# A new written order from the second group on, and one store per row tile, in a linear attention and FFN kernel

## The chip, the cores and the metric

The kernel runs on one core of a Trainium2 chip. The metric is the device time of one execution in microseconds, median over runs. Engine names are those of the profile: PE (TensorE, matmuls; PEld is its weight load), DVE (VectorE), ACT (ScalarE), POOL (GpSimd) and SP (SyncE, which here only issues DMAs; SPq is its queue).

## What is computed

A lightning (linear, decaying) attention over `q, k, v` of shape (4, 8, 768, 64), and behind it an FFN with a "snake" activation over its 3072 rows of 512. Cut to what matters:

```python
for b in range(nb):                       # blocks of 64 positions
    intra = einsum('bhic,bhjc->bhij', qb, kb) * Dmask
    intra = einsum('bhij,bhjd->bhid', intra, vb)
    inter = einsum('bhid,bhde->bhie', qb * lam_pow, kv_state)
    out[:, :, sl] = intra + inter
    kv_state = lam_block * kv_state + einsum('bhsd,bhse->bhde', kb * rev_pow, vb)

x = out.transpose(0, 2, 1, 3).reshape(B * S, H * D)        # 3072 x 512
h = x @ w_in                                               # 512 -> 2048
g = h + sin(alpha * h) ** 2 / (alpha + 1e-9)
return g @ w_out                                           # 2048 -> 512
```

## The kernel before

**Tiling.** The kernel takes chunks of 128 positions, in windows of 256. A *unit* is one batch entry, one half of the heads (4 of 8) and one window; there are 24. Four units (two batch entries, two halves of the heads) make a *group* of 512 rows; there are 6 groups, 0 to 5, and group g holds units 4g to 4g+3. Attention makes the group's transposed activations `xt`; FFN1 turns them into 16 tiles of hidden features (`f`), each 128 x 512, in PSUM; sine, square and a last VectorE step (`snake`) make `gall` of them; FFN2 makes four row tiles (`m`) of 128 rows of output from the 16, in four parts (`j`) of four matmuls each.

A chunk's 128 positions are loaded as 64 pairs (`two`), so position 2i lies on partition i of the half `par` 0 and position 2i+1 on partition i of the half 1. In the kernel before, this order of the positions is kept up to the output: a row tile holds the even rows on partitions 0 to 63 and the odd ones on 64 to 127.

**The written order.** There is no scheduler at run time and none at build time: `ORDER` (L18 to L128) is a list of items that are issued one after the other, each to one engine, and each engine works through its own items in that order. Waits come from the data and from buffers that have to come free. An item is `name.indices:engine:banks`, with V for VectorE, A for ScalarE, G for GpSimd, T for TensorE and S for SyncE. The names, with the lines of the kernel before:

| item | what it is | line |
|---|---|---|
| `ld.u.j` | load of q, k or v (j) of unit u, 256 KB | L259 |
| `sq`, `sk`, `cv` | scale q (QL), scale k (KD), cast v (VB), to bf16 | L300, L282/L284 |
| `tq`, `tk`, `tcq`, `tck` | transposes on TensorE (units 0 to 7) and their copies to QT | L327, L282/L284 |
| `tdq`, `tdk` | the same as DMA transposes from SP's queue (units 8 to 23) | L345 |
| `s`, `m.u.h` | scores, 64x64 matmuls into banks s0 and s1; their masking | L368, L378 |
| `k`, `kc`, `a`, `n` | K-by-V sums (`kvp`), their copy, the sum with the state (kvx) and its spread form (kvbd), the next state | L400, L282/L284, L421 and L425, L433 |
| `oi`, `o`, `x.u.c` | product with the state, with the masked scores, both into banks oa and ob; eviction into `xt` | L446, L460, L471 |
| `f1a`, `f1` | FFN1: `f1a` is the first half of the columns (first two units), `f1` the rest or all | L482 |
| `sin`, `sqr`, `stt` | sine, square, snake | L502, L509/L511, L516 |
| `f2.g.m.j`, `oc.g.m`, `st` | FFN2, copy of a row tile to an output buffer `ob`, its store | L525, L282/L284, L540 |
| `w.n:bank` | n warm-up matmuls on zeros, 256 columns each | L588 |
| `lt.i`, `ltc.i` | the last row tile, in three column pieces of 256, 128 and 128: matmuls, copy and store | L550, L560 |

**What ties them.** PSUM has eight banks (h0 to h3, s0, s1, oa, ob, numbered 0 to 7 in the items), each holding one tile at a time: a matmul into a bank waits until the tile before it in that bank has been read. The load buffers hold 8 units, KD and VB 5, QL and QT 4; there are 4 output buffers, which are reused in the order in which their stores stand. All loads, all DMA transposes and nearly all stores stand in SP's one queue; w_in and w_out come from GpSimd's. The loads of unit 4 and later are held until FFN1 tile 12 of group 0 (`HOLD`).

Of the kernel before, what the change touches and what calls it, by code (L numbers as in the profile page):

```python
# [18 lines left out]
tab:V ld.0.0:S sq.0:V ap:T w.4:T:h0 tq.0:T:0 ld.0.1:S ld.0.2:S sk.0:V cv.0:A w.3:T:h1 tk.0:T:5 al:V  # L19
tck.0:V ld.1.0:S ld.1.1:S ld.1.2:S ld.2.0:S ld.2.1:S ld.2.2:S ld.3.0:S tcq.0:A k.0:T:1,2 a.0.0:V  # L20
w.4:T:oa s.0:T sq.1:G sk.1:G sq.2:G kc.0.0:A kc.0.1:V m.0.0:V w.3:T:oa tq.1:T:2 w.3:T:oa tk.1:T:4
cv.1:A tcq.1:A k.1:T:0,1 oi.0:T m.0.1:V o.0:T x.0.0:A x.0.1:A tck.1:V kc.1.0:V kc.1.1:A a.1.0:V
s.1:T sk.2:V cv.2:A w.5:T:h2 tq.2:T:6 tk.2:T:1 w.2:T:h2 k.2:T:2,0 ld.3.1:S m.1.0:V m.1.1:V kc.2.0:V
kc.2.1:V wi.0:G wi.1:G a.2.0:V sq.3:G sk.3:G n.2.0:G wi.2:G n.0.0:G tcq.2:A w.1:T:ob oi.1:T tck.2:A
ld.3.2:S o.1:T x.1.0:A x.1.1:A cv.3:A s.2:T tq.3:T:1 w.4:T:oa oi.2:T tk.3:T:0 w.2:T:h2 k.3:T:2,3
m.2.0:V m.2.1:V o.2:T tck.3:V wi.3:G wo.0:G wo.1:G tcq.3:A s.3:T x.2.0:A a.3.0:V kc.3.0:V m.3.0:V
x.2.1:A m.3.1:V w.6:T:h1 oi.3:T f1a.0.0:T:0 f1a.0.1:T:4 o.3:T x.3.0:A kc.3.1:V f1a.0.2:T:3
f1a.0.3:T:2 wo.2:G x.3.1:V f1.0.0:T f1.0.1:T sin.0.0:A sin.0.1:A f1.0.2:T sqr.0.0:V stt.0.0:V
sqr.0.1:G stt.0.1:V f1.0.3:T f1.0.4:T:5 f1.0.5:T:7 sin.0.2:A sin.0.3:A sqr.0.2:A stt.0.2:V sqr.0.3:A
sin.0.4:A sqr.0.4:V sin.0.5:A f1.0.6:T:1 stt.0.3:V sin.0.6:A sqr.0.5:G f1.0.7:T:6 stt.0.4:V  # L30
f1.0.8:T:0 sqr.0.6:V stt.0.5:V stt.0.6:V f1.0.9:T:2 f1.0.10:T:4 f1.0.11:T:3 sin.0.7:A sin.0.8:A
sqr.0.7:G stt.0.7:V sqr.0.8:A stt.0.8:V n.1.0:G sin.0.9:A sqr.0.9:V a.1.1:G stt.0.9:V sin.0.10:A
sqr.0.10:G sin.0.11:A sqr.0.11:V f1.0.12:T:1 sin.0.12:A sqr.0.12:A a.0.1:G wo.3:G a.2.1:G n.2.1:G
stt.0.10:V stt.0.11:V f1.0.13:T:5 f1.0.14:T:7 sin.0.13:A sin.0.14:A n.0.1:G n.1.1:G n.3.0:G ld.4.0:S
ld.4.1:S ld.4.2:S ld.5.0:S ld.5.1:S ld.5.2:S ld.6.0:S sqr.0.13:V stt.0.12:V stt.0.13:V sqr.0.14:A
stt.0.14:V ld.6.1:S ld.6.2:S ld.7.0:S ld.7.1:S ld.7.2:S ld.8.0:S ld.8.1:S f2.0.0.0:T:0 f1.0.15:T:2
f2.0.0.1:T f2.0.1.0:T:6 sq.4:G f2.0.3.0:T:3 sin.0.15:A sqr.0.15:V f2.0.2.0:T:1 f2.0.1.1:T f2.0.2.1:T
stt.0.15:V f2.0.2.2:T f2.0.0.2:T f2.0.0.3:T f2.0.3.1:T oc.0.0:V a.3.1:G sk.4:G tq.4:T:7 tk.4:T:2
ld.8.2:S ld.9.0:S ld.9.1:S ld.9.2:S tck.4:V tcq.4:A f2.0.1.2:T s.4:T ld.10.0:S cv.4:A sq.5:G
tq.5:T:0 sk.5:G sq.6:G tcq.5:A f2.0.1.3:T oc.0.1:A sk.6:G tk.5:T:2 cv.5:G m.4.0:V f2.0.3.2:T m.4.1:V  # L40
k.4:T:6,7 a.4.0:V tck.5:A s.5:T m.5.0:V tq.6:T:0 cv.6:A tcq.6:V kc.4.0:A tk.6:T:2 m.5.1:V kc.4.1:A
ld.10.1:S ld.10.2:S f2.0.2.3:T tck.6:A oi.4:T k.5:T:0,2 o.4:T oc.0.2:A x.4.0:A x.4.1:A sq.7:G sk.7:G
s.6:T a.5.0:V kc.5.0:A kc.5.1:A f2.0.3.3:T tq.7:T:1 m.6.0:V m.6.1:V tcq.7:V cv.7:G n.3.1:G oi.5:T
oc.0.3:A sq.8:G tk.7:T:4 n.4.0:G sk.8:G tck.7:V a.4.1:G o.5:T k.6:T:0,2 k.7:T:1,3 x.5.0:A x.5.1:A
s.7:T n.5.0:G tdq.8:S a.6.0:V w.2:T:oa oi.6:T kc.6.0:A o.6:T a.7.0:V f1a.1.0:T:0 x.6.0:A m.7.0:V
n.4.1:G ld.11.0:S tdk.8:S ld.11.1:S x.6.1:A kc.6.1:V f1a.1.1:T:2 cv.8:A kc.7.0:A m.7.1:V oi.7:T
o.7:T k.8:T:4,5 f1a.1.2:T:1 x.7.0:V x.7.1:A f1.1.0:T f1.1.1:T f1.1.2:T kc.8.0:A sq.9:G f1a.1.3:T:4
f1.1.3:T kc.7.1:A f1.1.4:T:7 sin.1.0:A sin.1.1:A sin.1.2:A sk.9:G ld.11.2:S sqr.1.0:V stt.1.0:V
sin.1.3:A cv.9:A sqr.1.1:G stt.1.1:V sq.10:G sin.1.4:A sqr.1.2:V sqr.1.3:A stt.1.2:V stt.1.3:V
kc.8.1:V f1.1.5:T:3 sin.1.5:A f1.1.6:T:0 sqr.1.4:G sqr.1.5:G f1.1.7:T:6 f1.1.8:T:1 k.9:T:4,5  # L50
sin.1.6:A stt.1.4:V stt.1.5:V sin.1.7:A f1.1.9:T:2 kc.9.0:V sqr.1.6:A f1.1.10:T:7 kc.9.1:A sqr.1.7:A
tdq.9:S s.8:T a.8.0:G sk.10:G st.0.0.0:S ld.12.0:S tdk.9:S st.0.0.1:S stt.1.6:V stt.1.7:V sin.1.8:A
sqr.1.8:A sin.1.9:A sin.1.10:A stt.1.8:V m.8.0:V f1.1.11:T:3 f1.1.12:T:0 f1.1.13:T:1 sq.11:G
tdq.10:S sin.1.11:A f1.1.14:T:4 ld.12.1:S ld.12.2:S ld.13.0:S sqr.1.9:V sqr.1.10:A sqr.1.11:G
stt.1.9:V stt.1.10:V sin.1.12:A sqr.1.12:G sin.1.13:A stt.1.11:V stt.1.12:V m.8.1:V sk.11:G
f1.1.15:T:2 cv.10:G sin.1.14:A sqr.1.13:A oi.8:T sin.1.15:A tdk.10:S f2.1.0.0:T:3 sqr.1.14:A sk.12:G
sq.12:G f2.1.0.1:T f2.1.0.2:T a.9.0:G sqr.1.15:A cv.11:A stt.1.13:V stt.1.14:V stt.1.15:V s.9:T
o.8:T tdq.11:S ld.13.1:S ld.13.2:S k.10:T:0,1 x.8.0:A x.8.1:A m.9.0:V tdk.11:S f2.1.0.3:T m.9.1:V
oi.9:T kc.10.0:A st.0.1.0:S ld.14.0:S kc.10.1:A o.9:T cv.12:A x.9.0:A s.10:T k.11:T:2,0 f2.1.1.0:T:1
m.10.0:V a.10.0:G x.9.1:A kc.11.0:A kc.11.1:A m.10.1:V oi.10:T k.12:T:2,0 n.6.0:G n.8.0:G n.9.0:G  # L60
s.11:T o.10:T kc.12.0:V f2.1.1.1:T ld.14.1:S m.11.0:V ld.14.2:S n.10.0:G x.10.0:V m.11.1:V
f2.1.1.2:T ld.15.0:S st.0.1.1:S ld.15.1:S tdq.12:S ld.15.2:S ld.16.0:S ld.16.1:S ld.16.2:S ld.17.0:S
oc.1.0:A kc.12.1:A x.10.1:A a.11.0:G sk.13:G cv.13:G oi.11:T o.11:T x.11.0:A sq.13:G f2.1.1.3:T
sq.14:G oc.1.1:A n.7.0:G x.11.1:V f1.2.0:T:6 sin.2.0:A f1.2.1:T:5 sin.2.1:A sqr.2.0:A stt.2.0:V
ld.17.1:S st.1.1.0:S a.6.1:G n.6.1:G sk.14:G ld.17.2:S st.0.3.0:S st.0.2.0:S f1.2.2:T:2 sin.2.2:A
sqr.2.1:A stt.2.1:V f1.2.3:T:7 sin.2.3:A f1.2.4:T:0 f1.2.5:T:3 sin.2.4:A f1.2.6:T:4 f1.2.7:T:5
sqr.2.2:G stt.2.2:V sqr.2.3:A a.5.1:G stt.2.3:V sin.2.5:A f1.2.8:T:6 f1.2.9:T:7 f1.2.10:T:1 sq.15:G
sk.15:G sqr.2.4:A sin.2.6:A sqr.2.5:A stt.2.4:V f2.1.2.0:T:0 stt.2.5:V cv.14:G f1.2.11:T:3 tdk.12:S
f1.2.12:T:2 sin.2.7:A f2.1.2.1:T st.0.2.1:S sin.2.8:A sqr.2.6:G sqr.2.7:A stt.2.6:V sin.2.9:A
stt.2.7:V sqr.2.8:G sin.2.10:A n.11.0:G stt.2.8:V sqr.2.9:A sqr.2.10:A stt.2.9:V stt.2.10:V sq.16:G  # L70
sin.2.11:A sqr.2.11:A tdq.13:S n.5.1:G tdk.13:S tdq.14:S st.0.3.1:S tdk.14:S a.7.1:G a.12.0:G s.12:T
k.13:T:6,7 kc.13.0:A sin.2.12:A kc.13.1:A sqr.2.12:A m.12.0:V m.12.1:V tdq.15:S f1.2.13:T:1
f2.1.2.2:T sin.2.13:A sqr.2.13:A oi.12:T s.13:T o.12:T stt.2.11:V f2.1.2.3:T a.13.0:G m.13.0:V
stt.2.12:V m.13.1:V stt.2.13:V x.12.0:A x.12.1:A f2.1.3.0:T:3 n.13.0:G n.7.1:G a.8.1:G oi.13:T
sk.16:G oc.1.2:A f1.2.14:T:2 o.13:T k.14:T:1,0 s.14:T sin.2.14:A x.13.0:V x.13.1:V m.14.0:V n.8.1:G
sq.17:G n.12.0:G kc.14.0:A f2.1.3.1:T m.14.1:V f2.1.3.2:T sqr.2.14:A a.14.0:G kc.14.1:A tdk.15:S
ld.18.0:S ld.18.1:S oi.14:T ld.18.2:S sq.18:G cv.15:A cv.16:G cv.17:A k.15:T:1,0 o.14:T s.15:T
tdq.16:S tdk.16:S stt.2.14:V kc.15.0:V x.14.0:V x.14.1:A f1.2.15:T:2 f2.1.3.3:T st.1.2.0:S a.15.0:G
m.15.0:V kc.15.1:V oi.15:T m.15.1:V ld.19.0:S ld.19.1:S ld.19.2:S s.16:T ld.20.0:S st.1.0.0:S o.15:T
x.15.0:V k.16:T:1 x.15.1:V sin.2.15:A sqr.2.15:A m.16.0:V oc.1.3:V stt.2.15:V a.11.1:G f2.2.0.0:T:0  # L80
f1.3.0:T:7 kc.16.0:A st.1.0.1:S ld.20.1:S m.16.1:V sin.3.0:A sqr.3.0:A f1.3.1:T:4 f1.3.2:T:6
sin.3.1:A f1.3.3:T:1 sqr.3.1:A sin.3.2:A sin.3.3:A f1.3.4:T:5 sin.3.4:A f1.3.5:T:2 f1.3.6:T:3
sk.17:G st.1.2.1:S ld.20.2:S sk.18:G sk.19:G f2.2.0.1:T f2.2.0.2:T a.9.1:G sq.19:G sq.20:G sqr.3.2:G
stt.3.0:V sqr.3.3:A stt.3.1:V a.16.0:G n.9.1:G sin.3.5:A sqr.3.4:A stt.3.2:V n.14.0:G n.15.0:G
sin.3.6:A stt.3.3:V stt.3.4:V sqr.3.5:A ld.21.0:S tdq.17:S tdk.17:S sqr.3.6:A cv.18:G tdq.18:S
tdk.18:S st.1.3.0:S f1.3.7:T:1 oi.16:T stt.3.5:V a.10.1:G s.17:T o.16:T x.16.0:V k.17:T:2 f2.2.0.3:T
cv.19:G m.17.0:V stt.3.6:V x.16.1:V kc.17.0:A f2.2.1.0:T:2 a.17.0:G n.10.1:G n.11.1:G sk.20:G
cv.20:G a.12.1:G f2.2.1.1:T tdq.19:S ld.21.1:S tdk.19:S ld.21.2:S ld.22.0:S st.1.1.1:S tdq.20:S
ld.22.1:S tdk.20:S m.17.1:V oi.17:T oc.2.0:V s.18:T st.1.3.1:S k.18:T:3 k.19:T:0 o.17:T kc.18.0:A
# [41 lines left out]
def kernel(  # L131
# [11 lines left out]
    nc = tc.nc  # L143
    P = nc.NUM_PARTITIONS

    B, H, S, D = q.shape
    C = 128
# [234 lines left out]
    okv = {}  # L382
# [243 lines left out]
```

## Time and profile before

| what | us |
|---|---|
| six runs: 215.9, 216.45, 216.68, 214.27, 215.25, 216.06; median | 215.98 |
| the profiled execution's own time | 214.85 |
| its span, first to last instruction | 213.1 |
| PE busy | 206.1 |
| POOL busy | 141.4 |
| DVE busy | 129.6 |
| ACT busy | 123.6 |
| 96 snakes on DVE, mean 0.742 each | 68.2 |
| 96 sines on ACT, mean 0.688 each | 63.2 |
| 35 squares on POOL, mean 1.045 each | 36.3 |
| 46 stores of half a row tile, issue on SP's queue, median each | 0.587 |

The granted TensorE clock was 1.00. A row of a group reads: line, engine, operation, output<-input, shape, count, busy time and mean of one, then the idle time before it and who ended it. A row of waits reads: engine, line and tile that waited, what it waited for, total, number and longest. In the slices each digit is the busy share of a fortieth of the span (5.3 us) in tenths. In the chain and in the timeline a row begins with its start and its length in us; several instructions on end are merged into one row (x16).

### The profile page before, as it was taken

How to read it: one execution, taken by the hardware profiler on the slowest of the kernel's cores; microseconds unless marked ns; L12 is line 12 of the kernel's file. 1: busy time of each engine (PE TensorE's matmuls, PEld its weight loads, DVE VectorE, ACT ScalarE, POOL GpSimd, SP SyncE). 2: the span in 40 equal slices, each digit the busy share in tenths (PEclk: the TensorE clock that was granted, in tenths of full speed). 3: DMA queues.
4: the chain of work that ended last, by engine and by line, in shares of the span. 5: the costliest groups of instructions: out<-in, count | busy, mean ns of one | idle time of the engine just before them, and what ended most of it. 6: DMA issues, size and time to landing. Idle time of an engine off the chain costs nothing.

```text
span 213.1 us, 5493 instructions
## 1 busy us (share of the span) xinstructions
PE 206.1 (97%) x2132; PEld 109.7 (51%) x2132; DVE 129.6 (61%) x235; ACT 123.6 (58%) x244; POOL 141.4 (66%) x208
## 2 busy tenths in 40 slices
PE   7989999999999999999999999999999999999993
PEld 5668544457744554455444644444454444444463
DVE  3885897159599845778767694726884625532120
ACT  3563983077899839986494496926635659131001
POOL 5488389699797999999999987709841738030000
PEclk9999999999999999999999999999999999999999
DMA  5999999999999999969899899920520000172624
GB/s 138 294 242 181 203 204 273 281 289 290 207 194 205 243 210 282 246 114 196 227 256 118 197 163 234 103 49 0 123 53 3 0 0 0 39 158 52 149 49 99
DMA packets 64009, 33.92 MB, mean 159 GB/s; under 512 B 19680, under 2 KB 61040, under 8 KB 63984
## 3 DMA queue, kind: packets, MB, share of 16 engines
q1 hardware_dynamic: 59568, 29.31, 63.4%
q0 software_dynamic: 4224, 4.19, 12.3%
q8 instruction: 16, 0.26, 0.6%
q10 hardware_dynamic: 192, 0.07, 0.1%
q14 instruction: 9, 0.07, 0.1%
HBM read 27.28 MB, written 6.29 MB: 158 GB/s over the span
## 4 chain that ended last, share of the span: by engine, by line
PE 74%; DMA 11%; POOL 5%; ACT 3%; SPq 2%; issue 2%; DVE 1%; POOLq 0%; ACTq 0%
PE ops L525 32%; PE hps L482 30%; DMA w_out_sb<-in_moe_w_out_dram 4%; PE okv L460 3%; DMA st_q<-in_q_dram 3%; DMA QT<-KD 2%; PE sp L368 2%; ACT s L502 2%; SPq L259 2%; PE ops L550 2%; PE okv L446 2%; POOL QL L300 2%; DMA st_k<-in_k_dram 1%; POOL KD L300 1%; PE kvp L400 1%
## 5 line engine op out<-in xcount | busy, mean ns | idle before, releaser
L482 PE MATMUL hps<-xt,w_in_sb 128*128 128x512 bf16 (+1 forms) x416 | 87.5, 363 | 0.0
L525 PE MATMUL ops<-w_out_sb,gall 128*128 128x512 bf16 x368 | 85.9, 380 | 0.5 <-DMA w_out_sb<-in_moe_w_out_dram 0.5
L516 DVE SCALAR_TENSOR_TENSOR gall<-s,r_sb,hps 128x512 bf16<-128x512 bf16 x96 | 68.2, 742 | 23.5 <-POOL s L511 11.9
L502 ACT ACTIVATE s<-hps,alpha_sb 128x512 bf16<-128x512 f32 x96 | 63.2, 688 | 25.8 <-PE hps L482 25.1
L482 PEld LDWEIGHTS <-w_in_sb 128*128 128x128 bf16 x416 | 39.8, 98 | 40.7
L511 POOL TENSOR_TENSOR s<-s 128x512 bf16<-128x512 bf16 x35 | 36.3, 1045 | 35.3 <-ACT s L502 34.6
L525 PEld LDWEIGHTS <-gall 128*128 128x128 bf16 x368 | 34.6, 98 | 40.1 <-issue 0.8
L378 DVE TENSOR_TENSOR ST<-sp,mask 128x512 bf16<-128x512 f32 x48 | 31.8, 683 | 4.4 <-PE sp L368 4.2
L509 ACT ACTIVATE s<-s 128x512 bf16<-128x512 bf16 x51 | 31.5, 632 | 1.0 <-DVE gall L516 0.4
L300 POOL TENSOR_TENSOR QL<-st_q,E 128x512 bf16<-128x512 f32 x23 | 23.9, 1042 | 5.5 <-DMA st_q<-in_q_dram 3.4
L284 DVE COPY ob<-ops 128x512 f32<-128x512 f32 (+1 forms) x13 | 8.6, 658 | 29.5 <-PE ops L525 23.3
L300 POOL TENSOR_TENSOR KD<-st_k,R 128x512 bf16<-128x512 f32 x22 | 22.9, 1042 | 1.8 <-DMA st_k<-in_k_dram 1.5
L425 POOL TENSOR_TENSOR kvbd<-kvx,LBD 128x256 bf16<-128x256 f32 x32 | 19.6, 613 | 2.5
L282 ACT COPY ob<-ops 128x512 f32<-128x512 f32 (+2 forms) x13 | 7.1, 546 | 22.4 <-PE ops L550 12.0
L282 ACT CAST xt<-okv 128x256 bf16<-128x256 f32 x29 | 9.8, 374 | 11.6 <-PE okv L460 10.8
L421 POOL TENSOR_TENSOR kvx<-kva,kvs 128x128 f32<-128x128 f32 x32 | 14.7, 460 | 1.1 <-ACT kva L282 0.9
L284 DVE CAST xt<-okv 128x256 bf16<-128x256 f32 x19 | 7.7, 419 | 10.8 <-PE okv L460 10.8
L282 ACT COPY kva<-kvp 128x128 f32<-128x128 f32 x26 | 6.4, 273 | 9.2 <-PE kvp L400 8.2
L282 ACT COPY QT<-pt 128x512 bf16<-128x512 bf16 x9 | 5.2, 583 | 9.7 <-PE pt L327 9.7
L368 PE MATMUL sp<-QT 64*64 64x128 bf16 x384 | 9.9, 220 | 0.8 <-DMA QT<-KD 0.8
L460 PE MATMUL okv<-ST,VB 64*64 64x128 bf16 x384 | 9.9, 220 | 0.0
L282 ACT CAST VB<-st_v 128x512 bf16<-128x512 f32 x14 | 8.6, 623 | 2.0 <-DMA st_v<-in_v_dram 2.0
(57 smaller groups left out, 126.3 us busy)
## 6 DMA issues: line engine op xcount, KB each, us to landing
st_q<-in_q_dram SPq DMA_DIRECT2D x24, 256.0 KB, 5.1
st_k<-in_k_dram SPq DMA_DIRECT2D x24, 256.0 KB, 4.8
st_v<-in_v_dram SPq DMA_DIRECT2D x24, 256.0 KB, 5.0
out_dram<-ob SPq DMA_DIRECT2D x46, 128.0 KB, 2.5
w_in_sb<-in_moe_w_in_dram POOLq DMA_DIRECT2D x4, 512.0 KB, 7.9
w_out_sb<-in_moe_w_out_dram POOLq DMA_DIRECT2D x4, 512.0 KB, 12.5
QT<-QL SPq DMA_TRANSPOSE x16, 3.4
QT<-KD SPq DMA_TRANSPOSE x16, 3.8
```

Of the source, the lines that this page charges most:

```text
L282: nc.scalar.copy(out=out, in_=in_)
L284: eng.tensor_copy(out=out, in_=in_)
L300: eng.tensor_tensor(out=t[:], in0=stage[u, j][:].rearrange("p h two e -> p two h e"), in1=tab[:, :, hh * HH:(hh + 1) * HH].unsqueeze(3).to ...
L378: nc.vector.tensor_tensor(out=stm[u][:, hd], in0=sps[u][hd][:], in1=mask[:].unsqueeze(2).to_broadcast([P, 2, 2, P]), op=ALU.mult)
L425: eng.tensor_tensor(out=kvbd[u, c][:], in0=x.unsqueeze(2).to_broadcast([P, 2, 2, D]), in1=LBD[:, 2 * hh:2 * hh + 2, :].unsqueeze(3).to_bro ...
L460: nc.tensor.matmul(out=okv[u][c][half[hd], hp * P:(hp + 1) * P], lhsT=VB[half[c], par, 2 * hp + hd, :], rhs=ST[half[c], hd, par, hp, :], s ...
L482: f1mm[g, f] = nc.tensor.matmul(out=hps[g, f][:].rearrange("p (b i) -> p b i", b=2)[:, bs] .rearrange("p b i -> p (b i)"), lhsT=w_in_sb[:, ...
L502: nc.scalar.activation(out=s1[g, f][:], in_=hps[g, f][:], func=ACTF.Sin, scale=alpha_sb[:, f:f + 1])
L509: nc.scalar.activation(out=s2[g, f][:], in_=x[:], func=ACTF.Square)
L511: eng.tensor_tensor(out=s2[g, f][:], in0=x[:], in1=x[:], op=ALU.mult)
L516: nc.vector.scalar_tensor_tensor(out=gall[g][:, f, :], in0=s2.pop((g, f))[:], scalar=r_sb[:, f:f + 1], in1=hps.pop((g, f))[:], op0=ALU.mul ...
L525: nc.tensor.matmul(out=ops[g, m][:], lhsT=gall[g][:, f, m * P:(m + 1) * P], rhs=w_out_sb[:, f, :], start=(f == 0), stop=(f == NFC - 1))
```

## The change

Three edits:

1. The written order is another one from group 1 on, with smaller differences in group 0. Squares go from GpSimd (35 to 30) to ScalarE (51 to 56); copies of the K-by-V sums from ScalarE (26 to 19) to VectorE (14 to 21); two row-tile copies and two evictions from VectorE to ScalarE; banks are chosen anew. Warm-ups are 42 matmuls in 11 items (39 in 12 before).
2. The eviction into `xt` puts the two halves of a chunk back in the order of the positions: it writes every second bf16 element, in two passes of 64 for each head pair.
3. So a row tile has its 128 rows on 128 partitions in order, and is stored by one DMA of 256 KB and not by two of 128 KB with every second row. The last tile's three pieces go by one DMA each (the second on ScalarE's queue).

```diff
 # group 1's attention, TensorE's items alone
-s.7:T w.2:T:oa oi.6:T o.6:T f1a.1.0:T:0 f1a.1.1:T:2 oi.7:T o.7:T k.8:T:4,5 f1a.1.2:T:1 f1.1.0:T
+s.7:T oi.6:T o.6:T w.4:T:s0 f1a.1.0:T:4 oi.7:T o.7:T f1a.1.1:T:2 f1a.1.2:T:3 f1.1.0:T
 # VectorE's items there
-m.5.0:V tcq.6:V m.5.1:V a.5.0:V m.6.0:V m.6.1:V tcq.7:V tck.7:V a.6.0:V a.7.0:V m.7.0:V
+m.5.0:V tcq.6:V m.5.1:V a.5.0:V kc.5.0:V m.6.0:V m.6.1:V tcq.7:V tck.7:V a.6.0:V a.7.0:V m.7.0:V
 # TensorE's items at the last chunk of w_out
-f2.0.0.2:T f2.0.0.3:T f2.0.3.1:T tq.4:T:7 tk.4:T:2
+f2.0.0.2:T tq.4:T:0 f2.0.0.3:T f2.0.3.1:T tk.4:T:5
 # SP's queue, units 16 to 20
-tdq.16:S tdk.16:S st.1.2.0:S ld.19.0:S ld.19.1:S ld.19.2:S ld.20.0:S st.1.0.0:S st.1.0.1:S ld.20.1:S
-st.1.2.1:S ld.20.2:S ld.21.0:S tdq.17:S tdk.17:S tdq.18:S tdk.18:S st.1.3.0:S tdq.19:S ld.21.1:S tdk.19:S
+tdq.16:S st.1.0.0:S tdk.16:S ld.18.0:S ld.18.1:S ld.18.2:S ld.19.0:S ld.19.1:S st.1.3.0:S tdq.17:S st.1.1.0:S
+tdk.17:S ld.19.2:S ld.20.0:S ld.20.1:S ld.20.2:S tdq.18:S tdk.18:S tdq.19:S
+ld.21.0:S ld.21.1:S ld.21.2:S ld.22.0:S ld.22.1:S ld.22.2:S ld.23.0:S ld.23.1:S tdk.19:S tdq.20:S tdk.20:S
 # the end
-oc.4.2:V oc.4.3:A st.4.3.0:S st.4.2.0:S st.4.3.1:S st.4.2.1:S oc.5.0:V st.5.0.0:S st.5.0.1:S
-oc.5.1:V st.5.1.0:S st.5.1.1:S lt.0:T:3 oc.5.2:V st.5.2.0:S lt.1:T:7 st.5.2.1:S ltc.0:A lt.2:T:5 ltc.1:A ltc.2:V
+oc.4.2:V oc.4.3:A st.4.3.0:S st.4.2.0:S oc.5.0:A
+oc.5.1:V oc.5.2:A lt.0:T:6 st.5.1.0:S lt.1:T:4 st.5.2.0:S st.5.0.0:S ltc.0:A lt.2:T:1 ltc.1:A ltc.2:V
...
     def outev(u, c, eng, **_):
...
-        copy(eng, xt[g][:, 2 * hh:2 * hh + 2, bb, c, :],
-             okv[u][c][:, 0:2 * P].rearrange("p (hp i) -> p hp i", hp=2))
+        copy(eng, xt[g][:, 2 * hh:2 * hh + 2, bb, c, :].rearrange(
+                 "p hp (i two) -> p hp two i", two=2),
+             okv[u][c][:, 0:2 * P].rearrange("p (hp two i) -> p hp two i", hp=2, two=2))
...
     def out_rows(g, m):
...
-        return out[r0:r0 + C].rearrange("(p two) d -> two p d", two=2)
+        return out[r0:r0 + C]
...
-    def store(g, m, par, **_):
-        nc.sync.dma_start(out=out_rows(g, m)[par], in_=obs[g, m][par * D:(par + 1) * D, :])
+    def store(g, m, _i, **_):
+        nc.sync.dma_start(out=out_rows(g, m), in_=obs[g, m][:])
...
     def last_copy(i, eng, **_):
...
-        for par, queue in ((0, nc.sync), (1, nc.scalar if i else nc.sync)):
-            queue.dma_start(out=rows[par][:, c0:c0 + n], in_=ob[par * D:(par + 1) * D, :])
+        (nc.scalar if i == 1 else nc.sync).dma_start(out=rows[:, c0:c0 + n], in_=ob[:])
```

## The prediction

> **What bounds the kernel now.** I read the page first, then TensorE's own waits, then the chain of work from the first wait to the last matmul, and last the queue that issues the DMAs. The page's engine row and its slices:
>
> ```profile
> PE 206.1 (97%) x2132; PEld 109.7 (51%) x2132; DVE 129.6 (61%) x235; ACT 123.6 (58%) x244; POOL 141.4 (66%) x208
> ...
> PE   7989999999999999999999999999999999999993
> ...
> POOL 5488389699797999999999987709841738030000
> ```
>
> TensorE is full from the second slice to the last, at full granted clock. POOL is nearly full too up to about the 24th slice (130 us), and the DMA engines with it (share 0.83 to 1.21 in stretches of that time, over 1 where queues overlap); later both run empty. So the time is the sum of TensorE's work, its waits, and a head and tail. TensorE's longest waits but one (in total, times, longest):
>
> ```profile
> PE sp L368 <- DMA QT<-KD: 0.8, 2, 0.5
> PE pt L327 <- POOL KD L300: 0.6, 1, 0.6
> PE ops L525 <- DMA w_out_sb<-in_moe_w_out_dram: 0.5, 1, 0.5
> ```
>
> The second, and two that are not shown (1.1 and 0.3), lie in the head, where little changes. After 18 us, 1.26 us of waiting is left: 0.51 for the last chunk of w_out (at 40.8), and 0.28 and 0.47 for two DMA transposes of K (scores of units 16 and 17, at 103.5 and 114.6). Nothing else of the middle can be gained but matmuls that cost less. How the later wait came about, in the chain (start, us, what) and in the DMA issue queue:
>
> ```profile
> 101.41 3.19 DMA st_k<-in_k_dram
> 104.61 1.00 POOL KD L300
> ...
> 109.24 5.30 DMA QT<-KD
> 114.55 0.04 issue
> 114.59 0.42 PE sp L368 x16
> ```
>
> ```profile
> 107.92 1.22 SPq L345 DMA_TRANSPOSE QT<-QL  x1
> 109.24 1.22 SPq L345 DMA_TRANSPOSE QT<-KD  x1
> ```
>
> Unit 17's K is scaled by 105.6, its transpose is issued at 109.2 behind loads and stores, and it lands 5.3 us later. At the tail, the copy of tile 2 of the last group and the last copy of all:
>
> ```profile
> 206.11 0.69 DVE L284 COPY ob<-ops 128x512 f32<-128x512 f32 x1 [2.82 <-PE ops L525]
> ...
> 209.59 0.29 DVE L284 COPY ob<-ops 128x128 f32<-128x128 f32 x1 [2.79 <-PE ops L550]
> ```
>
> The profiled execution took 214.85 us (span 213.1 and 1.75 around it). The six runs have a median of 215.98, so it is 1.13 shorter than the median; I sum against 214.85 and come back to that.
>
> **The change, step by step.**
>
> *Fewer store issues.* 46 half stores become 23, at a median of 0.587 us of SP's queue each: 13.5 us of issuing leave a queue that between 60 and 130 us hardly rests. SP is on no path but through its transposes, so this is worth what the next term says and nothing by itself.
>
> *Transposes against scores.* I add up POOL's work in the written order by its rows (1.04 for a scaling or a square, 1.07 for a decay with its sum, 0.40 and 0.61 for the rest) from unit 4's scaling at 35.94, and TensorE's by its pieces from 18.04 (0.86 for four matmuls of 512, 0.22 and 0.12 for a small block), and take the distance from the end of a unit's K scaling to its scores. Before, units 16 and 17 have 8.4 and 11.2, and those two waited; others have 11 to 29 (unit 11 has 9.1 and did not wait). After, they have 16.8 and 22.5, and the smallest is unit 11 with 11.3. On SP, eleven loads and stores and the Q transpose stood between unit 16's and unit 17's K transpose; now seven, and the Q transpose. From unit 16's Q transpose to unit 20's K transpose SP now issues ten transposes at 1.22, 17 loads at 0.55 and three stores, 23.3 us; it may start at about 98 us (when TensorE is done with unit 12's QT buffer) and is through by 122, plus a landing of 3.8, against scores of unit 20 at about 135. Both waits go: -0.75. What is late next is not a transpose.
>
> *w_out.* The transposes of unit 4's Q (4 matmuls, 0.22) stand ahead of the first matmul on the last chunk now: -0.22 of the 0.51, if QL of unit 4 is there (36.98 in this trace). Bounds 0 and -0.51.
>
> *Changes of matmul kind.* A block of 64x64 matmuls costs more when it follows 128x128 ones, and the other way round:
>
> ```profile
> 70.92 0.35 PE sp L368 x16
> 71.27 0.22 PE okv L460 x16
> 71.49 0.12 PE kvp L400 x16
> 71.61 0.97 PE ops L525 x4
> ...
> 88.27 0.86 PE ops L525 x4
> ```
>
> That is 0.13 in and 0.11 out. From the first FFN2 matmul on there are 25 such round trips before and 27 after: +0.48. The useful matmuls are the same.
>
> *The end of group 1's attention.* Here the new order is tighter. On VectorE, the copy of unit 5's kv sums (0.28, on ScalarE before) stands ahead of unit 6's masks; in the trace unit 7's scores begin at 51.38, just behind the copy of its K (50.59 + 0.74 = 51.33). So they come some 0.27 later, in part hidden, as the next step waits for ScalarE's copies until 51.9 in either order. Then a warm-up of 4 matmuls and the first FFN1 block of group 1 use the bank s0, which unit 7's first mask must have read. In the trace that mask ends at 52.78; with 0.28 ahead of it, at 53.06. Warm-up (0.43) until 53.5, half a block of FFN1 (0.43), unit 7 (0.56), two more halves (0.86): the first second-half block starts at 55.35 instead of 54.57: +0.8. Unit 8's kv matmuls, 0.12, come after that point now, not ahead of it: +0.12. Bounds: +0.2 (only the longer warm-up, if the mask is in time) and +1.2 (if the mask also waits its turn for one copy of 0.42). I take 0.92, since the mask's place behind the two kvbd products (0.76) is the same in both orders. Behind TensorE everything waits there.
>
> *Evictions with a step.* The 48 copies of okv into xt write every second bf16. No row shows a stepped write. Nearest rows: the same copy without a step, 419 ns on VectorE and 374 on ScalarE, and one of twice the elements, 688 and 588. They could cost nothing (my value: the reading side, float32 from PSUM, is unchanged) or up to 0.27 each. A gain I exclude, since nothing gets smaller. Those within a group lie behind other matmuls. At three group edges TensorE waits for the last one: between unit 11's last product and FFN1 lies 0.97 of other work, and both evictions stand on VectorE: 0.84 against 0.97, or 1.38 and a wait of 0.4. So 0 to +1.2.
>
> The page "SBUF — State Buffer" of the Trainium skill, in its section on the DMA port swizzle, has lines of 16 bytes and says that up to 8 bf16 of step are free; by it the 4-byte step costs nothing. No run here shows that yet.
>
> *Other banks and buffers.* For every bank I took the TensorE time between its last matmul and the next that overwrites it. For FFN1 banks (sine 0.69, square 0.63 or 1.04, then 0.74 on VectorE) the smallest is 3.24 before, with no wait; after, 2.94 and 2.99. 0.69 + 0.63 + 0.74 is 2.06, so I take 0, bounds 0 and +0.4.
>
> *The tail.* SP's last issue starts at once after the last copy, not 0.1 later: -0.1. But the order of the stores is tile 1, tile 2, tile 0 now, and output buffers are reused in the order of release, so the last copy takes tile 2's buffer and waits for tile 2's store. That copy ends (0.09 + 0.585 on ScalarE) 0.68 after its matmuls; the last tile's matmuls need 3.55 (1.77, 0.89, 0.89). So the store, 256 KB, has 2.87 us to land. Half a store lands in 2.4 (median); a load of 256 KB in 5.1, among full DMA engines. The tail's engines are half empty, so I take the nearer row, 2.4 and a little, no wait; the bound is 5.1 - 2.87 = +2.2.
>
> "DMA: Bandwidth & Descriptors" of the Trainium skill (section "Anatomy of one DMA — SWDGE (gpsimd) path") makes a DMA a fixed 2.0 us, mostly the receipt of the write, plus bytes at 436 GB/s, measured on the other issuing path. By it 256 KB would land after an estimated 2.6 us and the copy would not wait; doubled by the rows of the loads it would wait 2.2. The 128 KB row of 2.4 agrees with it (2.3).
>
> **Sum.** -0.75 - 0.22 + 0.48 + 0.92 - 0.1 = +0.33: 215.2 on the profiled execution's scale. For a median, the 1.13 that other runs took longer has to be placed. No view shows where it lies. If it is late transposes, it goes with the short distances, and the median is 215.2; if it is the head, w_out or the chip, it stays: 216.3. Of the three waits after 18 us the transposes have 0.75 of 1.26, so I lean to the first: **215.4**.
>
> **Rivals.**
> - *Faster.* The mask of unit 7 is in time (+0.2, not +0.92) and the 1.13 goes: 214.5; with all of the w_out wait gone 214.2. For it: POOL loses five squares (5.2 us) and SP 13.5 us of issues. Against it: TensorE itself has more to do, not less.
> - *Slower, by the last copy.* It waits for tile 2's store. At a landing of 5.1 it costs 2.2: 217.4, or 218.5 if the 1.13 stays. It decides alone from a landing of 4.7 on (215.2 + 1.86 = 217.06); if the 1.13 stays, from 3.6. Against it: stores' largest landing is 4.9, but in the busy middle.
> - *Slower, by stepped evictions.* At 688 ns, +1.2 at the edges, and FFN1 banks gain no slack: 216.4 to 217.5.
> - *The change does not do what it says:* the waits move to other units. Then -0.75 is lost: 216.0, no change.
>
> **How the numbers follow.** About 0.5% (1.08 us) is what a measurement of this kernel can tell from no change; the bounds are 214.9 and 217.06. Forecast, with the rival of moved waits: 0.43, own range 214.9 to 216.5. Faster rival 0.31. Last copy 0.13, stepped evictions 0.13. So faster 0.31, same 0.43, slower 0.26. Range: from 214.2 to 217.4, which leaves out the worse half of the last two.
>
> **What would show it.** TensorE's waits for QT at scores gone; the w_out wait at 0.3; a new wait of some 0.5 ahead of the warm-up before group 1's FFN1; 48 xt copies with unchanged means (419, 374); the last copy straight behind its matmuls; SP's stores 23 at about 0.59. I am wrong if the xt rows grow, if the last copy waits for a DMA, or if runs of the new kernel spread by 2.4 us as these do (214.27 to 216.68).

## The result, and the profile after

The changed kernel takes 217.14 us (median of 30 executions, 216.39 to 218.71), the kernel before beside it 215.84 (65 executions, 213.88 to 218.68). The ratio is 1.0082, with a 95% interval of 1.0065 to 1.0098: 0.8% slower, where 215.4 and no change were forecast. (The ratios leave out executions over 1.5% above the fastest of the same kernel; the kernel before has many of these, so a ratio lies somewhat above that of the two medians.)

The profiled execution took 217.94 us, its span 216.0. The page's engine row and slices:

```profile
PE 208.0 (96%) x2135; PEld 110.3 (51%) x2135; DVE 129.9 (60%) x239; ACT 127.9 (59%) x245; POOL 136.8 (63%) x203
...
PE   8989999799799999999999999999999999999994
...
POOL 6497289599919995998969988784762056130000
```

TensorE is busy 1.9 us longer than before (208.0 against 206.1) and falls to 7 tenths in two slices in which it had 9, the eighth (38 to 43 us) and the eleventh (54 to 59). POOL has its five squares less. TensorE's waits:

```profile
PE ops L524 <- DMA w_out_sb<-in_moe_w_out_dram: 1.1, 1, 1.1
...
PE okv L444 <- ACT xt L280: 0.8, 2, 0.6
PE hps L481 <- DVE xt L282: 0.6, 2, 0.3
...
PE bz L586 <- DVE ST L376: 0.2, 1, 0.2
```

The waits of scores for QT are gone, as forecast. The last row is the forecast wait of the warm-up for a mask, 0.2 where I had 0.5. New, and not forecast at all, are two rows in which TensorE waits for evictions into `xt` (lines 469 to 471 of the changed kernel, recorded under its helper's lines 280 and 282). What do these wait for themselves? The groups of the eviction, first of after, then of before (busy time, mean ns | idle time ahead of them and what ended it):

```profile
L280 ACT CAST xt<-okv 128x256 bf16<-128x256 f32 x31 | 12.8, 449 | 24.2 <-PE okv L458 18.0 <-PE hps L481 6.2
L282 DVE CAST xt<-okv 128x256 bf16<-128x256 f32 x17 | 7.4, 443 | 14.3 <-PE okv L458 10.1 <-PE hps L481 4.2
```

```profile
L282 ACT CAST xt<-okv 128x256 bf16<-128x256 f32 x29 | 9.8, 374 | 11.6 <-PE okv L460 10.8 <-PE kvp L400 0.7
L284 DVE CAST xt<-okv 128x256 bf16<-128x256 f32 x19 | 7.7, 419 | 10.8 <-PE okv L460 10.8
```

Two things differ. One eviction takes 449 ns on ScalarE (374 before) and 443 on VectorE (419). And five times the engine sat idle ahead of one, 10.4 us in all, until `hps` matmuls ended, that is FFN1, which *reads* `xt`. Before, evictions waited for the product that they evict. The timeline around group 1's first FFN1 blocks, TensorE alone, and below it ScalarE's evictions:

```profile
53.69 0.42 PE L458 MATMUL okv<-ST,VB 64*64 64x128 bf16 x16
...
54.93 0.60 PE L481 MATMUL hps<-xt,w_in_sb 128*128 128x256 bf16 x4
56.15 0.27 PE L444 MATMUL okv<-QT,kvbd 128*128 128x128 bf16 x2 [0.62 <-ACT xt L280]
...
58.29 1.92 PE L481 MATMUL hps<-xt,w_in_sb 128*128 128x256 bf16 x16 [0.32 <-DVE xt L282]
```

```profile
55.34 0.76 ACT L280 CAST xt<-okv 128x256 bf16<-128x256 f32 x2 [1.90 <-PE hps L481]
57.79 0.44 ACT L280 CAST xt<-okv 128x256 bf16<-128x256 f32 x1 [1.56 <-PE hps L481]
```

The half block at 54.93 reads the columns of units 4 and 5. The two evictions at 55.34 write those of unit 6. Their product is done at 54.11 (the first line) and ScalarE has been idle for 1.90 us, but they start only when that half block is done, 1.2 us after their product. They free the bank that unit 7's product needs, so TensorE waits 0.62 for it. The same happens to unit 7 (57.79, then 0.32 at 58.29) and in group 0 to unit 3. By 58.29 the trace is 3.7 us behind that of before at the like place, with some 0.4 of it from the very start.

Further on it regains 0.4: the transposes' 0.75 is there, against dearer matmuls. Unit 17's K transpose is issued later than before (114.07 against 109.24), but its scores stand at 124.7:

```profile
110.76 2.63 SPq L343 DMA_TRANSPOSE QT<-QL  x1
113.44 0.57 SPq L539 DMA_DIRECT2D out_dram<-ob  x1
114.07 1.21 SPq L343 DMA_TRANSPOSE QT<-KD  x1
```

At the tail, the last copy follows its matmuls (they end at 212.86) and waits for no store; the copy before it waited 0.52 for one, beside other work:

```profile
212.00 0.27 ACT L280 COPY ob<-ops 128x128 f32<-128x128 f32 x1 [0.52 <-DMA out_dram<-ob]
...
212.95 0.29 DVE L282 COPY ob<-ops 128x128 f32<-128x128 f32 x1 [6.35 <-PE ops L549]
```

From the last matmul to the end of the span it takes 3.1 us (3.5 before).

### The profile page after: what moved, and what is told of

The parts are those of the page before. It is cut to its first block, busy times and chain, and to the rows that moved or that the text cites. A ratio compares the mean times of both kernels' runs of the same rounds, so it can differ in the third digit from the quotient of the medians.

```text
span 216.0 us, 5448 instructions
## 1 busy us (share of the span) xinstructions
PE 208.0 (96%) x2135; PEld 110.3 (51%) x2135; DVE 129.9 (60%) x239; ACT 127.9 (59%) x245; POOL 136.8 (63%) x203
## 4 chain that ended last, share of the span: by engine, by line
PE 80%; DMA 7%; POOL 3%; ACT 2%; DVE 2%; SPq 2%; issue 2%; DVEq 0%; ACTq 0%; POOLq 0%
PE ops L524 34%; PE hps L481 34%; DMA w_out_sb<-in_moe_w_out_dram 4%; PE okv L458 3%; DMA st_q<-in_q_dram 3%; PE sp L366 3%; PE okv L444 2%; PE kvp L398 2%; PE ops L549 2%; ACT s L501 2%; SPq L257 2%; PE pt L325 1%; POOL QL L298 1%; POOL w_in_sb L267 1%; PE bz L586 1%
## 5 line engine op out<-in xcount | busy, mean ns | idle before, releaser
L510 POOL TENSOR_TENSOR s<-s 128x512 bf16<-128x512 bf16 x30 | 31.1, 1047 | 39.3 <-ACT s L501 37.9
L508 ACT ACTIVATE s<-s 128x512 bf16<-128x512 bf16 x56 | 34.1, 630 | 1.2 <-DVE gall L515 0.4
L280 ACT CAST xt<-okv 128x256 bf16<-128x256 f32 x31 | 12.8, 449 | 24.2 <-PE okv L458 18.0
L280 ACT COPY ob<-ops 128x512 f32<-128x512 f32 (+2 forms) x15 | 8.2, 549 | 22.2 <-PE ops L524 20.6
L282 DVE COPY ob<-ops 128x512 f32<-128x512 f32 (+1 forms) x11 | 7.1, 649 | 23.0 <-PE ops L524 16.7
L431 POOL TENSOR_TENSOR kvs<-kvx,LHP 128x128 f32<-128x128 f32 x24 | 9.4, 399 | 0.0
L444 PEld LDWEIGHTS <-kvbd 128*128 128x128 bf16 x80 | 6.4, 98 | 5.6 <-issue 1.0
```

The costliest lines, as they stand in the source:

```text
L280: nc.scalar.copy(out=out, in_=in_)
L508: nc.scalar.activation(out=s2[g, f][:], in_=x[:], func=ACTF.Square)
L510: eng.tensor_tensor(out=s2[g, f][:], in0=x[:], in1=x[:], op=ALU.mult)
```

## The experiments

The first theory, W: the evictions' waits for FFN1 are no waits for data. FFN1's half block reads the first two units' part of `xt`, the evictions write the other two units' part; but where the view of the write is rearranged, it is taken to overlap, and a wait is put in when the program is built. The rival, S: the stepped write itself is the cost, by its longer rows. A third: the new order is slower by itself. Runs 1 to 4 were on one chip, 5 to 12 on a second and 13 to 15 on a third; each is compared with executions of before beside it.

**1. The new order without the step (e1_plain).**

```diff
-        copy(eng, xt[g][:, 2 * hh:2 * hh + 2, bb, c, :].rearrange(
-                 "p hp (i two) -> p hp two i", two=2),
-             okv[u][c][:, 0:2 * P].rearrange("p (hp two i) -> p hp two i", hp=2, two=2))
+        copy(eng, xt[g][:, 2 * hh:2 * hh + 2, bb, c, :],
+             okv[u][c][:, 0:2 * P].rearrange("p (hp i) -> p hp i", hp=2))
```

> The changed kernel with the old eviction into xt (no step) and everything else as changed; left out: the rows of each row tile are stored in the wrong order. Theory W (the stepped write makes an eviction wait for the FFN1 half blocks that read other columns of the same xt tile, seen as 6.2 and 4.2 us of xt waiting for hps in groups 0 and 1): these waits vanish, so do TensorE's 0.62 and twice 0.32 at the two group edges, and the last w_out chunk is issued some 0.5 earlier; 1.5 to 2.2 faster than the changed kernel, about 215.2. Theory O (the new order's own tight places: bank s0, the masks of unit 7, two more changes of matmul kind): within 0.4 of the changed kernel, about 217. Theory S (the stepped write only takes longer, 449 for 374 ns): 0.2 to 0.5 faster, about 216.7.

Measured: 215.12 us (before there: 216.66), ratio 0.9953 (0.9919 to 0.9987). TensorE has no wait for `xt`, and neither eviction waits for `hps`:

```profile
L280 ACT CAST xt<-okv 128x256 bf16<-128x256 f32 x31 | 10.8, 375 | 22.5 <-PE okv L458 22.4
L282 DVE CAST xt<-okv 128x256 bf16<-128x256 f32 x17 | 7.1, 421 | 11.6 <-PE okv L458 11.6
```

Against the changed kernel's 217.14 (on another chip) the eviction alone, step and view together, is worth 2 us, and the new order with one store is not slower than before.

**2. The step and the one store in the old order (e2_bstep).** The order stays that of before; a store item with `par` 0 stores the whole tile, one with `par` 1 nothing.

> The order of before with the stepped eviction and one store per row tile (correct rows). W: the evictions of units 3, 6 and 7 wait for FFN1 half blocks here too, 1 to 2 slower than before, 217 to 218. O: as before or up to 0.4 faster, 215.4 to 215.9. S: 0.1 to 0.3 slower.

Measured: 216.33, ratio 0.9987 (0.9954 to 1.0019). The waits for `hps` came (1.9 and 3.7 us of idle time, four evictions), and still it was no slower than before. Half a miss: something in this run paid for them; run 5 shows what can have.

**3. The step on the reading side (e3_read).** The same result, written in one piece and read from PSUM with a step:

```diff
         copy(eng, xt[g][:, 2 * hh:2 * hh + 2, bb, c, :].rearrange(
-                 "p hp (i two) -> p hp two i", two=2),
-             okv[u][c][:, 0:2 * P].rearrange("p (hp two i) -> p hp two i", hp=2, two=2))
+                 "p hp (i two) -> p hp i two", two=2),
+             okv[u][c][:, 0:2 * P].rearrange("p (hp two i) -> p hp i two", hp=2, two=2))
```

> The changed kernel, but the eviction reads PSUM with a step of 64 elements and writes xt without one; the same result. W: no xt waits for hps, time as without the step at all, about 215.2, if the stepped read costs no more than the 449 ns. O: about 217. S: depends on the row: at 374 ns as e1.

Measured: 217.41, ratio 1.0029 (0.9999 to 1.0059). The rows are those of an unstepped copy, but the waits stayed:

```profile
L280 ACT CAST xt<-okv 128x256 bf16<-128x256 f32 x31 | 10.8, 374 | 24.8 <-PE okv L458 18.3 <-PE hps L481 6.3
L282 DVE CAST xt<-okv 128x256 bf16<-128x256 f32 x17 | 7.1, 422 | 14.2 <-PE okv L458 10.1 <-PE hps L481 4.1
```

This run parts W from S: with no price of a step left, the kernel is as slow as the changed one, and 2.29 us slower than run 1 on the same chip. It also corrects W, by which the waits would have gone (215.2): the addresses written here are the same as in run 1, and only the view by which they are named is different. So the wait comes with the rearranged view of `xt`, not with the step.

**4. The same in the old order (e4_bread).** The edits of runs 2 and 3 together.

> The order of before, with the stepped read and one store per row tile; the same result. W: no xt waits for hps; what is left is 23 issues less on SP's queue: 0 to 0.8 faster than before, if the waits for transposes (0.75) hang on that queue. O: the same number. If it is slower than before, the stepped read is what costs.

Measured: 215.98, ratio 0.9978 (0.9944 to 1.0012), again with the waits (1.9 and 3.7 us of idle time). The time was expected, its composition was not.

**5. One store per tile alone (e5_bone).** The order and the eviction of before:

```diff
-        return out[r0:r0 + C].rearrange("(p two) d -> two p d", two=2)
+        return out[r0:r0 + C]
...
-        nc.sync.dma_start(out=out_rows(g, m)[par], in_=obs[g, m][par * D:(par + 1) * D, :])
+        if par == 0:
+            nc.sync.dma_start(out=out_rows(g, m), in_=obs[g, m][:])
...
```

Not shown: the three pieces of the last tile go by one DMA each, too, as in the changed kernel.

> The order of before and its contiguous eviction, with one store per tile; the rows of the output come out permuted, since the step that sorts them is left out. The 23 store issues that go lie on a queue that is on no path but through the two transposes that TensorE waited for (0.28 and 0.47 us), so: 0 to 0.8 us faster than before (ratio 0.996 to 1.000), no wait for xt. If one store per tile were a cost of its own (256 KB landing late, the last copy waiting for tile 2's store), this run would be slower than before.

Measured: 213.66 us (213.42 to 214.06; before there: 216.29), ratio 0.986 (0.9821 to 0.9899). The sign is right, the size three times my upper bound. TensorE's waits in its profile:

```profile
PE bz L564 <- DVE warm L193: 1.1, 1, 1.1
PE ops L525 <- DMA w_out_sb<-in_moe_w_out_dram: 0.6, 1, 0.6
PE pt L327 <- POOL KD L300: 0.4, 2, 0.3
PE pt L327 <- POOL QL L300: 0.2, 1, 0.2
PE kvp L400 <- ACT VB L282: 0.2, 1, 0.2
```

No scores wait for QT, in the order in which they did. On SP's queue unit 17's pair of transposes now starts 2.3 to 2.9 us earlier than in the profile of before (107.92 and 109.24 there):

```profile
105.04 1.85 SPq L345 DMA_TRANSPOSE QT<-QL  x1
106.99 1.21 SPq L345 DMA_TRANSPOSE QT<-KD  x1
```

A whole store holds SP's queue for 0.43 us (median of 23), a half one for 0.59 (median of 46), so some 17 us of issuing go, where I had counted 13.5. Of the 2.63 us, two things are seen beside the longer profiles of before in runs 11 and 12: their waits for QT (1.1 and 1.4), and 0.4 from the last matmul to the end (3.1 against 3.5). The rest, 0.8 to 1.1, is not placed.

**6, 7, 8. Another layout of xt (e6_lread, e7_lwrite, e8_blread).** The dimension of the two units of a half goes outermost, so that what is written lies apart from what FFN1's half blocks read, however the view is written:

```diff
-            xt[g] = xtp.tile([P, HP, 2, 2, P], BF16, name="xt")
-        copy(eng, xt[g][:, 2 * hh:2 * hh + 2, bb, c, :].rearrange(
+            xt[g] = xtp.tile([P, 2, HP, 2, P], BF16, name="xt")
+        copy(eng, xt[g][:, bb, 2 * hh:2 * hh + 2, c, :].rearrange(
...
-                rhs=xt[g][:, c, bs].rearrange("p b c i -> p (b c i)"),
+                rhs=xt[g][:, bs, c].rearrange("p b c i -> p b (c i)"),
```

The first has the new order and the step on the reading side, the second the new order and the step on the writing side as in the changed kernel, the third the old order and the step on the reading side.

> The changed kernel with two edits to the eviction: xt's dimension of the two units of a half is put outermost, so that what an eviction writes lies apart from what the half blocks of FFN1 read, however its view is written; and the step is on the reading side, so the rows are those of the unstepped copy (374 and 422 ns in the run with the step on the reading side). Theory 'the evictions of units 3, 6 and 7 of a pass wait for FFN1 matmuls that never read what they write': those waits go (evictions end their idle time behind okv again), and the time is that of the order with the contiguous eviction, 215.1, ratio 0.995 (0.992 to 0.999). Theory 'the new order itself is slower where the evictions stand, the step only showed it': 216.5 to 217.4 as with the step on the reading side alone.

> The same layout of xt, but with the step on the writing side as in the changed kernel. Against the run with the step on the reading side this is the price of the stepped write alone: 48 copies at 449 (ScalarE) and 443 ns (VectorE) in place of 374 and 422. If the price lies beside TensorE's work: as that run, within 0.3 us. If the last eviction of each group holds TensorE: six group edges by up to 0.15 us, up to 0.9 us slower than that run. The waits of evictions for FFN1's matmuls are gone here too if they come from the view.

> The order of before with the same layout, the step on the reading side and one store per tile: all of the change but the order, without the waits for FFN1's matmuls. Against the run with one store and the contiguous eviction in this order it should be the same within 0.3 us; against the run with the new order and the same eviction it is the worth of the new order: my sum gives that order -0.75 for two transposes, -0.22 for w_out, +0.48 for two round trips of matmul kind, +0.92 for the end of group 1's attention and -0.1 at the tail, +0.33 in all. Theory 'the order is worth more than summed, since group 1's edge cost nothing in the run of the new order with the contiguous eviction': this run is 0.3 to 0.9 us slower than that one with the new order.

Measured, on the chip of run 5 (before 216.29): e6_lread 215.02, ratio 0.9977 (0.9943 to 1.001); e7_lwrite 215.56, ratio 0.9946 (0.9918 to 0.9974); e8_blread 213.69, ratio 0.9874 (0.9829 to 0.9918). In e6_lread the evictions wait for their own product again, and the rows are short:

```profile
L280 ACT CAST xt<-okv 128x256 bf16<-128x256 f32 x31 | 10.8, 375 | 22.2 <-PE okv L458 22.1
L282 DVE CAST xt<-okv 128x256 bf16<-128x256 f32 x17 | 7.1, 421 | 11.6 <-PE okv L458 11.6
```

That agrees with W: the view is rearranged as before, and once what is written lies apart from what is read, no wait is put in. (That the build takes the view's overlap too wide is my reading of runs 1, 3 and 6; they show what the wait goes with, not how it is computed.)

By the medians of the one chip, the stepped write is worth 0.54 (e6_lread to e7_lwrite), but this is not clear of the noise: the executions lie at 214.71 to 216.49 and 214.85 to 216.59, their means are 0.22 apart, and the two ratios to before stand the other way round. In e7_lwrite's profile TensorE waits 0.2 for an eviction, in e6_lread's not at all.

The old order with all of the rest (e8_blread) is 1.33 faster than the new one (e6_lread). My sum had it 0.33 faster, and the theory that I had put against the sum had it 0.3 to 0.9 slower: that theory is refuted, and the sum, which credits the new order with the -0.75 of the transposes, is too small. It keeps the rows of the output in place, and beats the kernel before by 1.3%: it is the version that one would keep. Against e4_bread, which has the same but the layout, it is 2.3 faster, though on another chip: if the chips are alike, the waits cost no less in the old order than in the new one, and in runs 2 and 4 this hid the gain of run 5.

**9. Two half stores of rows that follow each other (e9_halves).**

```diff
-        return out[r0:r0 + C].rearrange("(p two) d -> two p d", two=2)
+        return out[r0:r0 + C].rearrange("(two p) d -> two p d", two=2)
```

> The kernel before with one word changed: each of the two stores of a tile writes 64 rows that follow each other, in place of every second row. The rows of the output come out permuted; the number of issues (46), their bytes and their places in the order stay. One store per tile in this order took 213.7 us where before took 216.3, and its executions lay within 0.7 us where those of before spread over 4.9. Theory 'issues on SP': 46 issues at 0.587 us stay, so the time and the spread stay as before, 215.5 to 216.5. Theory 'every second row': what costs is writing rows with gaps, and this run takes 213.4 to 214.4.

Measured: 216.5 (214.89 to 220.46; before there: 216.3), ratio 0.9997 (0.9954 to 1.004). No price of rows with gaps is seen, and scores wait 1.5 us for QT in its profile: it is two stores in place of one that cost.

**10. The new order with the old stores and eviction (e10_ahalf).**

> The new order with the eviction and the two half stores of before (both issued at the place of the one). With the runs of before's order with two stores (216.3), with one (213.7), and of the new order with one (215.0 and 215.1) this makes a square. Theory 'the new order has slack, which half stores eat': its longer distances between transposes and scores cover what 23 more issues delay, so 215.0 to 215.6, and within 2 us from lowest to highest. Theory 'half stores cost as much in any order': 215.1 + 2.6 = 217.7, and as wide a spread as before.

Measured: 217.38 (before there: 216.3), ratio 1.0082 (1.0046 to 1.0118): by its number the second theory, by its profile the first (the spread, 2.4 us, fits neither well). No scores wait for QT, and TensorE's last matmul ends at 210.17 (209.99 in e6_lread). What is lost shows at the tail, where the last copy waits for a half store and SP's queue is longer (below, the same queue in e6_lread):

```profile
210.02 2.45 SPq L559 DMA_DIRECT2D out_dram<-ob  x4
210.69 0.29 DVE L282 COPY ob<-ops 128x128 f32<-128x128 f32 x1 [6.78 <-DMA out_dram<-ob]
```

```profile
208.63 2.10 SPq L558 DMA_DIRECT2D out_dram<-ob  x2
```

The copy starts 0.5 us after the last matmul (0.1 in e6_lread), and SP's last issue ends at 212.47 in place of 210.73. From the last matmul to the end it takes 4.7 us, 1.6 more than in e6_lread; the medians are 2.4 apart, and the rest is not seen in this profile. So either part of the change alone takes the waits for QT away. Of the profiles in the old order, the four with two stores on SP's queue (before and runs 9, 11 and 12) have them, 0.8 to 1.5 us, and the four with one store (runs 2, 4, 5 and 8) have none; in the new order no profile has them, with one store or with two. Together the two parts take them away once.

**11, 12. The kernel before, two more profiles (b2_before, b3_before).**

> The kernel before, unchanged, for one more profile of it: its executions lie between 213.9 and 218.8 us, and the one profile so far is of a short one (214.85). What the longer ones wait for is not seen in any view yet. If it is late transposes, scores of TensorE wait for QT for 0.75 + 1.4 us in an execution of 216.3; if it is the head or w_out, the first FFN1 block starts later than 18.04 or the wait for w_out is longer than 0.51.

> The kernel before once more, for a third profile: the same expectations as for the second. Where the three differ in time, the difference should stand in the waits for QT at scores, if late transposes make the spread.

Measured: 216.25 and 216.38 us, 1.4 and 1.5 above the profile that I predicted from. Their TensorE waited for QT 1.1 and 1.4 (0.8 there), where 2.15 was expected if late transposes were all. The second (b3_before), in TensorE's waits and in its chain:

```profile
PE sp L368 <- DMA QT<-KD: 1.4, 2, 1.1
PE bz L564 <- DVE warm L193: 1.1, 1, 1.1
PE kvp L400 <- POOL kvx L421: 0.7, 1, 0.7
```

```profile
102.32 3.28 DMA st_k<-in_k_dram
105.60 1.00 POOL KD L300
...
110.23 5.60 DMA QT<-KD
115.87 0.42 PE sp L368 x16
```

The chain is that of the first profile, a microsecond later. The rest of the difference stands in other single waits (kvx 0.7 here; in the other one 0.4 for `gall`), and in no one place.

**13. Half of the store issues on ScalarE's queue (e11_actq).**

```diff
-        nc.sync.dma_start(out=out_rows(g, m)[par], in_=obs[g, m][par * D:(par + 1) * D, :])
+        queue = nc.scalar if par else nc.sync
+        queue.dma_start(out=out_rows(g, m)[par], in_=obs[g, m][par * D:(par + 1) * D, :])
```

> The order of before and its two half stores per tile, with the second half issued on ScalarE's queue in place of SP's. SP then issues 23 stores, as with one store per tile; the transfers are the 46 of before. Theory 'SP's issuing delays the transposes': 213.5 to 214.8, no scores that wait for QT of unit 17, save what 23 issues cost ScalarE (58% busy). Theory 'the transfers themselves': 215.5 to 217, the waits for QT at scores of 0.75 to 1.5 us as in three profiles of before.

Measured: 222.48 (before there: 215.91), ratio 1.032 (1.0276 to 1.0365), outside both. No scores wait for QT, as in the first theory, but ScalarE's queue pays:

```profile
PE hps L482 <- DVE gall L516: 4.9, 3, 3.5
...
PE okv L446 <- ACT xt L282: 1.0, 1, 1.0
```

Stores there stand in line with sines and evictions, and those behind them come late, up to 3.5 us for one FFN1 bank. This also spoils the test of the waits for QT, as that wait lies just ahead of the scores of unit 17:

```profile
110.69 1.59 SPq L345 DMA_TRANSPOSE QT<-KD  x1
```

```profile
120.10 1.02 PE L482 MATMUL hps<-xt,w_in_sb 128*128 128x512 bf16 x4 [3.45 <-DVE gall L516]
...
121.28 0.42 PE L368 MATMUL sp<-QT 64*64 64x128 bf16 x16
```

The scores come 6.7 us later than in before's first profile (114.59), the transpose of K only 1.5 later (109.24 there). So neither theory is shown: whether it is the issuing on SP or the number of transfers that costs stays open.

**14, 15. The changed kernel and its twin with the other layout, on one chip (a2_after, e7b_lwrite).**

> The changed kernel again, beside the run with only the layout of xt changed (waits for FFN1's matmuls gone, stepped write kept), on one chip. On two chips they were at 217.1 and 215.6. If the waits that the view brings have that price: 1.2 to 2.0 us between the two here; if the two chips made the difference, less than 0.5.

> The partner of the run of the changed kernel on the same chip: the new order, the stepped write, one store per tile, and xt's dimension of the units outermost. 215.2 to 215.9, 1.2 to 2.0 us below the changed kernel.

Measured: 217.31 and 215.76 (before there: 215.91), ratios 1.0057 (1.0024 to 1.0089) and 0.9987 (0.9955 to 1.0019). The waits that come with the view cost 1.55 us, as expected; the pair of runs 1 and 3, which has no stepped write, has 2.29. In the two profiles TensorE waits 1.4 and 0.2 us for evictions, and 0.6 and 0.3 for `w_out`, so 1.5 of it is seen.

**The sum of the steps**, each between two medians of one chip:

| from | to | what | us |
|---|---|---|---|
| before 216.29 | e5_bone 213.66 | one store per tile | -2.63 |
| e5_bone 213.66 | e8_blread 213.69 | positions sorted by a stepped read, layout without waits | +0.03 |
| e8_blread 213.69 | e6_lread 215.02 | the new order | +1.33 |
| e6_lread 215.02 | e7_lwrite 215.56 | the step on the writing side | +0.54 |
| e7b_lwrite 215.76 | a2_after 217.31 | the old layout, with the waits | +1.55 |

Together +0.82, that is 217.11 from 216.29. The changed kernel was at 217.14 and 217.31, so the end fits. The start doesn't stand as still: before had medians of 215.8 to 216.7 in the five sets of runs. The first, third and fifth steps are clear of the noise; +0.03 and +0.54 are not.

## Why the prediction was wrong, by its own steps

**"Evictions with a step" is the step that failed.** I took 0, "the reading side, float32 from PSUM, is unchanged". It failed twice. As a size, the lesser part: the stepped write took 75 ns more on ScalarE and 24 on VectorE. By the medians that is 0.54 us in all, by the means 0.22, where my bounds were 0 to +1.2. The Trainium skill ("SBUF — State Buffer", on the DMA port swizzle), by which 4 bytes of step are free, did not hold for this write: 449 ns against 374. And as a kind: I asked how long an eviction takes, not what it has to wait for. That is where 1.55 us was: the evictions of units 3 and 7, at group edges, and of unit 6, one of those that "lie behind other matmuls", waited for matmuls that never read what they write. My list of what would show me wrong had "if the xt rows grow", which they did, but not this wait. Another of its signs came as well: executions of the new kernel spread by 2.3 us. The rival "stepped evictions" (216.4 to 217.5) holds the measured time by luck: it had rows of 688 ns, which did not come, and no wait for FFN1. The 1.74 us between 215.4 and 217.14 are about these two parts, 1.55 and 0.2 to 0.5. Without them the forecast is near, 215.0 to 215.1 (e6_lread and e1_plain), but in part by luck too: one store gained more than I had for the late transposes, and the order cost more, as follows.

**"Fewer store issues": worth "nothing by itself" was wrong.** Alone it is worth 2.63 us. I looked at the one profile, found 0.75 us of late transposes, and gave this to the new distances in the order. The stores alone would have done it, and more: the waits that one store removes differ from profile to profile (0.8 to 1.5 in four), and the tail gains 0.4. Some 1 us of the 2.63 is not placed.

**"Transposes against scores": right in the profile, credited to the wrong part.** The waits are gone in after. But as one store removes them in the old order too, the new order's own share of the -0.75 is nothing once the stores are whole. My sum without this term is +1.08 for the order, on the profiled scale; e8_blread to e6_lread measured +1.33. The times in this step were off as well, without a cost: I had SP's queue through with unit 20's K transpose by 122 us; in after it is issued at 131.5, for scores at 138.4.

**The 1.13 us between profile and median**: I leaned to late transposes that go away. They do. But two more profiles show that they are only part of it, and the new order gives about half of the gain back.

**"Changes of matmul kind": the rows fit +0.48.** The rows of scores, of the products with masked scores and of K-by-V sums grew by 0.2, 0.2 and 0.4 us from e5_bone to e6_lread, FFN2's shrank by 0.3: +0.5. The other profiles of the two orders show nearly the same rows.

**"The end of group 1's attention": right place, size too large.** The warm-up waits for the mask for 0.27 in e6_lread and 0.16 in after; with the two more warm-up matmuls (0.60 us for four against 0.39 for two) about 0.5, not 0.92. The parts known of the order add to about 1.0; it measured 1.33 by the medians and 1.25 by the means, so some 0.3 of it is noise or not placed.

**"w_out": not to be told.** TensorE's wait for it was 1.1 in after, 0.6 in its second profile, 0.3 in e6_lread and none in e1_plain, all with the same order there; the kernel before had 0.5, 0.7 and 0.2.

**"Other banks and buffers" and "The tail".** FFN1 banks cost nothing in after (one wait of 0.3 for `gall` in e7b_lwrite). The tail gained 0.4, where I had 0.1, and so it did with one store in the old order (e5_bone). The rival of the last copy did not happen: 256 KB landed after 2.3 us (median of 23; 2.87 were there). The estimate of 2.6 us that I worked out from the Trainium skill's page "DMA: Bandwidth & Descriptors" (on the anatomy of one DMA) was nearer to that than the row of the loads, 5.1; the row of the half stores, 2.4, by which I went, was nearest. With two half stores in the new order (e10_ahalf) that rival did happen, at 0.4 us.

## What to carry to other kernels

When an edit changes how an access is written, ask first what the instruction will now wait for and only then how long it takes: idle time of an eviction that is ended by the *readers* of its destination can be the mark of a wait that no data asks for, if they read other parts of the tile than it writes; putting what is written and what is read into separate outer blocks of the tile removed it here. Where a kernel's executions spread over several microseconds, one profile shows only a sample of its waits: take more than one before pricing the part that feeds them, here a DMA queue shared by stores and transposes. And when two parts of a change each cure the same wait, the cure counts once: here the new order, which costs 1.33 us once the stores are whole, can be left out.

## What the runs showed of the hardware that I had not expected

- Writing every second bf16 element (128x256 from float32 in PSUM) took 449 ns on ScalarE against 374 in one piece, but only 443 against 419 on VectorE. Reading the same float32 from PSUM with a step of 64 elements cost neither of them anything: 375 and 421.
- 46 half stores against 23 whole ones on a queue shared with loads and DMA transposes are worth 2.6 us of 216. The issue of a whole store held SP's queue for 0.43 us, that of a half one for 0.59 (medians). Six executions with whole stores spread over 0.6 us, but those of other kernels with whole stores over 1.7 to 3.0, against 4.9 of before (23 executions). Whether the rows of a half have gaps in DRAM made no difference that can be seen (216.5 against 216.3).
- With the second halves issued from ScalarE's queue the kernel took 222.5 us: 23 issues of about 0.48 us each, 11 us in all, on an engine that is busy for 58%, cost 6.6 us more than on SP.
